# Top-k attention with a maxout MLP: norms of the weights by products on TensorE, low halves from TensorE and ScalarE, loads ranked anew

## The chip, the core and the metric

One core of a Trainium2 chip runs the whole program. Its engines are TensorE (PE, with its weight loads PEld), VectorE (DVE), ScalarE (ACT), GpSimd (POOL) and SyncE (SP), which issues all DMA transfers of this kernel. The metric is the device time of one execution in microseconds.

## What is computed

```python
# q, k, v: (8, 8, 576, 64); top_k = 32
scores = scale * np.matmul(q, k.transpose(0, 1, 3, 2))
kth = np.partition(scores, -top_k, axis=-1)[..., -top_k:-top_k + 1]
scores = np.where(scores >= kth, scores, -1e9)
attn = softmax(scores)
x = np.matmul(attn, v).transpose(0, 2, 1, 3).reshape(4608, 512)
# w1, w2, w3: (512, 768), w_out: (768, 512); all inputs are float64 in memory
h = np.maximum(np.maximum(x @ w1, x @ w2), x @ w3)
out = h @ w_out
```

## The kernel before

The inputs lie in memory as 64-bit numbers. The attention is cut into 144 units of 128 rows for two heads. A unit's scores (`qk`, 12 matmuls) are evacuated by ACT (`evac`) and swept by DVE (`sweep`, 14 MAX8); DVE, POOL and ACT then find the 32nd largest of each row (`pivot`, `sign`, `window` on POOL, `below`, `place`, `pick`), DVE masks (`mask`), ACT takes exponentials (`expo`), PE transposes them (`turn`) and multiplies by v (`values`). `prep` makes q and k of a pair of heads: transposes on PE (`products`), a high part on ACT (`split`), the low part on POOL (line 479).

The MLP works on 576 tokens of a batch. Each float32 operand is a sum of two f16 halves, so each product is three matmuls (`layer`, line 767, for w1 to w3; `layer2`, line 827, for w_out). DVE takes the larger of the three (`largest`).

The weights come once, in 18 parts of 128 rows: 4 each for w1, w2, w3 (768 columns, 786 KB in memory), 6 for w_out (512 columns). They go through these steps:

- `load_weight` issues the DMA of a part on SP.
- `decode` makes float32 out of the 64-bit words, by three DVE instructions (lines 249 to 251) for each half of a part of w1 to w3, or for a whole part of w_out: 30 pieces, 90 instructions. Their result goes into `wall`, the tile of all weights.
- `square_w` squares a part on ACT (line 261); `sum_w` adds the squares up by columns, by two matmuls with ones on PE (line 270). `column_scale` takes the largest column sum on DVE (lines 280, 282), and `powers` makes a power of two of it, by which the matrix is scaled. For w_out the sum over all elements is used (`norm_scale`).
- `cut` makes the two halves, 256 columns at a time: a scaled float32 copy (ACT, line 307), the high half (ACT, line 310) and the difference of the two, the low half (POOL, line 313): 48 of each.

The order of all instructions is made in Python by `in_order`: each step is a `Piece` with an engine, an estimated cost, the pieces it needs, the rings of buffers it takes and a rank. A piece's rank is the unit's number plus an offset by kind (`OFFSETS`). The planner repeatedly takes the piece that could start first, with patience by engine (`PATIENCE`) and within `LEAD` units of rank; pieces marked `alone` wait for POOL and hold POOL back in the plan. MLP pieces are `fill`: PE takes them when nothing else could start. The engines then run what stands in their queue, in order. Two PSUM tiles (ring `m`) serve `layer`, `layer2` and the column sums.

Of the kernel before, what the change touches and what calls it, by code (L numbers as in the profile page):

```python
# [19 lines left out]
CUT = 256  # L20
# [7 lines left out]
GAP = 121.0  # L28
NEAR = 87.0
SWITCH = 95.0  # L30
WINDOW = 150
LEAD = 9.1
LOCK_A = -150.0
LOCK_B = -100.0
OFFSETS = {'E0': 1.08, 'E1': 1.7, 'E2': 0.44, 'N': -1.46, 'T0': 0.49, 'T1': 2.25, 'T2': 3.75, 'Y': -0.11, 'Z': 0.23, 'd': 1.26,
# [94 lines left out]
PATIENCE = {'PE': 121, 'DVE': 164, 'ACT': 32, 'POOL': 175, 'SP': 0}  # L130
# [3 lines left out]
def kernel(ctx, tc, q, k, v, moe_w1, moe_w2, moe_w3, moe_w_out, out):  # L134
# [70 lines left out]
    wosq = const.tile([P, FC], F32, name="wosq")  # L205
    ones_b = const.tile([P, P], BF16, name="ones_b")
    nc.vector.memset(ones_b, 1.0)
    columns = []
    raw_of = {}

    def halves(i, c, c0, n):

        at0 = 2 * ((i * KC + c) * DF + c0 // CUT * CUT) + c0 % CUT
        return [wall.bitcast(F16)[:, at0 + t * CUT:at0 + t * CUT + n] for t in range(2)]

# [4 lines left out]
    def load_weight(j):  # L220
# [7 lines left out]
        elif j < ODD:  # L228
            raw = [t[:, :n] for t in (spare if j % 4 == 1 else [h.bitcast(I32).rearrange("p f n -> p (f n)") for h in H])]
        elif j == len(parts) - 1:  # L230
            raw = [wk.tile([P, 2 * n], I32, name="ssb", bufs=NSSB)]
        else:
            raw = [spare[(j - ODD) // 2]]
# [5 lines left out]
    def decode(j, j0):  # L239

        src, c, n, at0 = parts[j]
        m, k0 = PIECE[n], j0
        raw = raw_of[j]
        if len(raw) == 2:
            raw, k0 = raw[j0 // m:], 0
# [908 lines left out]
```

## Time and profile before

| | |
|---|---|
| Median of 3 timed runs | 1306.12 us (1306.06 to 1307.36) |
| Profiled execution | 1304.12 us |
| its span, first to last instruction | 1301.9 us |
| PE busy | 1174.8 us (90%) |
| DVE busy | 1174.4 us (90%) |
| ACT busy | 1081.6 us (83%) |
| POOL busy | 954.0 us (73%) |
| mean granted clock of PE | 0.973 |

Busy time is what the engine's instructions took; a matmul's end is modelled, so a PE that is busy all the time need not be at its peak rate. Two engines with the same share can be needed at different times, so the stretches matter more than the sums. The granted clock is 1.00 at 2.4 GHz and 0.50 at 1.2 GHz.

### The profile page before, as it was taken

The numbers are of one execution on the slowest core, as the hardware profiler recorded it, in microseconds if no ns is written. First come the engines' busy times: TensorE is split into PE (matmuls) and PEld (weight loads), VectorE is DVE, ScalarE is ACT, GpSimd is POOL, SyncE is SP. The second block draws the span as 40 slices with busy tenths as digits, with TensorE's granted clock in tenths as the row PEclk, the third lists the DMA queues.
The fourth block names the chain that finished last, engine by engine and source line by source line (L and its number), as shares of the span: only waits on it lengthen the run. The fifth ranks groups of instructions, "written<-read, shape, count | busy, mean of one in ns | idle before, by whom it ended". The sixth has DMA issues, their size and how long they took to land.

```text
span 1301.9 us, 31770 instructions
## 1 busy us (share of the span) xinstructions
PE 1174.8 (90%) x10263; PEld 877.3 (67%) x10263; DVE 1174.4 (90%) x5561; ACT 1081.6 (83%) x2438; POOL 954.0 (73%) x1491
## 2 busy tenths in 40 slices
PE   3435878999789999999999999999999999999997
PEld 2223747877568676877777776777677776867775
DVE  7998898999999999999999999999999999999411
ACT  3779988898988899999988998888988898888421
POOL 4659688678877888888778787887787787767310
PEclk9997988999689999999999999999999999999999
DMA  6423112111101101111001111111111111000000
GB/s 200 146 73 109 45 27 47 39 45 37 47 11 28 45 15 50 35 38 47 19 27 39 39 36 42 29 45 29 29 45 28 46 27 37 2 18 2 17 17 28
DMA packets 112399, 54.83 MB, mean 42 GB/s; under 512 B 96608, under 2 KB 104800, under 8 KB 112224
## 3 DMA queue, kind: packets, MB, share of 16 engines
q1 hardware_dynamic: 112224, 52.72, 14.8%
q8 instruction: 83, 1.36, 0.4%
q14 instruction: 92, 0.75, 0.2%
HBM read 43.25 MB, written 9.44 MB: 40 GB/s over the span
## 4 chain that ended last, share of the span: by engine, by line
PE 58%; DVE 13%; ACT 3%; issue 1%; POOL 1%; DMA 0%; SPq 0%; DVEq 0%; POOLq 0%; ACTq 0%
PE m L767 23%; PE tr L710 8%; PE m L827 8%; PE s L518 8%; PE tr L679 7%; DVE L L535 3%; DVE ssb L624 3%; DVE Q L583 2%; PE tr L470 1%; DVE h L776 1%; PE tr L674 1%; ACT pm L633 1%; PE tr L676 1%; DVE z L564 1%; ACT w L574 1%
## 5 line engine op out<-in xcount | busy, mean ns | idle before, releaser
L579 POOL TENSOR_TENSOR w<-ssb,w 128x576 f32<-128x576 f32 x288 | 429.0, 1495 | 56.8 <-ACT w L574 54.2
L767 PE MATMUL m<-xh,wall 128*128 128x256 f16 (+4 forms) x2592 | 440.3, 273 | 2.5 <-DVE h L776 1.7
L767 PEld LDWEIGHTS <-wall 128*128 128x128 f16 x3888 | 352.5, 98 | 75.9 <-issue 11.2
L767 PE MATMUL m<-xl,wall 128*128 128x256 f16 (+4 forms) x1296 | 344.2, 272 | 0.0
L535 DVE MAX8 L<-ssb 128x8 f32<-128x82 f32 (+1 forms) x2016 | 316.3, 228 | 0.2 <-ACT ssb L526 0.2
L624 DVE SCALAR_TENSOR_TENSOR ssb<-ssb,kth 128x576 f32<-128x576 f32 x288 | 256.9, 906 | 1.8
L633 ACT ACTIVATE pm<-ssb,nb 128x576 f32<-128x576 f32 x288 | 223.8, 778 | 26.4 <-DVE ssb L624 25.6
L574 ACT ACTIVATE w<-ssb,Q 128x576 f32<-128x576 f32 x288 | 222.2, 775 | 22.7 <-DVE Q L567 18.8
L691 ACT COPY pT<-tr 128x512 f32<-128x512 f32 (+1 forms) x432 | 215.3, 513 | 22.1 <-PE tr L679 12.9
L583 DVE MAX8 Q<-w 128x8 f32<-128x576 f32 x288 | 215.5, 750 | 6.5 <-POOL w L579 6.3
L679 PE MATMUL tr<-ident,pm 128*128 128x128 f32 x1152 | 183.6, 286 | 24.2 <-ACT pm L633 16.2
L518 PE MATMUL s<-kT,qT 64*128 64x288 f32 x1920 | 179.1, 324 | 20.8 <-ACT ssb L526 11.6
L710 PE MATMUL tr<-pT,vt 128*64 128x256 f32 (+2 forms) x2000 | 182.3, 332 | 4.1 <-ACT pT L691 3.6
L518 PEld LDWEIGHTS s<-kT,qT 64*128 64x128 f32 x1920 | 142.5, 198 | 60.1 <-ACT ssb L526 20.0
L679 PEld LDWEIGHTS tr<-ident,pm 128*128 128x128 f32 x1152 | 133.9, 145 | 68.1 <-ACT pm L633 25.3
L526 ACT COPY ssb<-s 128x1152 f32<-128x1152 f32 x144 | 160.9, 1118 | 14.6 <-PE s L518 13.8
L776 DVE SCALAR_TENSOR_TENSOR h<-m,rises,h 128x256 f32<-128x256 f32 (+4 forms) x216 | 103.0, 477 | 69.0 <-PE m L767 64.7
L710 PEld LDWEIGHTS tr<-pT,vt 128*64 128x64 f32 x2000 | 113.3, 141 | 61.8 <-issue 16.6
L782 POOL TENSOR_TENSOR hl<-h,hh 128x256 f16<-128x256 f32 (+4 forms) x108 | 80.4, 745 | 77.1 <-ACT hh L779 75.8
L827 PE MATMUL m<-wall,hh 128*128 128x512 f16 x432 | 129.2, 380 | 1.6 <-POOL wall L313 1.1
L827 PE MATMUL m<-wall,hl 128*128 128x512 f16 x216 | 82.1, 380 | 0.0
L779 ACT CAST hh<-h 128x256 f16<-128x256 f32 (+4 forms) x108 | 43.6, 404 | 44.4 <-DVE h L776 43.9
(124 smaller groups left out, 1685.4 us busy)
## 6 DMA issues: line engine op xcount, KB each, us to landing
qt<-in_q_dram SPq DMA_DIRECT2D x72, 128.0 KB, 2.8
kt<-in_k_dram SPq DMA_DIRECT2D x72, 128.0 KB, 3.0
out_dram<-ob SPq DMA_DIRECT2D x32, 256.0 KB, 2.3
wall<-in_moe_w_dram SPq DMA_DIRECT2D x8, 768.0 KB, 5.6
vt<-in_v_dram SPq DMA_DIRECT2D x32, 128.0 KB, 2.4
vt<-in_v_dram SPq DMA_DIRECT2D x32, 64.0 KB, 2.2
vt<-in_v_dram SPq DMA_DIRECT2D x96, 16.0 KB, 2.0
vt<-in_v_dram SPq DMA_DIRECT2D x32, 48.0 KB, 2.1
```

The costliest lines, as they stand in the source:

```text
L518: nc.tensor.matmul(s[:, h, i, :HALF], qT[sl, qa, c0:c0 + P], kT[sl, ka, i * HALF:(i + 1) * HALF], start=(n_ == 0 and a == 0), stop=(n_ == ...
L535: nc.vector.max(d["L"][:, t, g, :], d["ssb"][t][:, g * S // G:(g + 1) * S // G])
L574: nc.scalar.activation(d["w"][t], d["ssb"][t], AF.Sign, bias=d["Q"][:, t, 0:1], scale=-1.0, accum_out=d["cnt"][:, t:t + 1])
L579: nc.gpsimd.tensor_tensor(d["w"][t], d["ssb"][t], d["w"][t], ALU.mult)
L583: nc.vector.max(d["Q"][:, t, 1:NW], d["w"][t])
L624: nc.vector.scalar_tensor_tensor(ss, ss, d["kth"][:, t:t + 1], ss, ALU.is_lt, ALU.subtract, accum_out=d["lost"][:, t:t + 1])
L633: nc.scalar.activation(d["pm"][:, t], d["ssb"][t], AF.Exp, bias=d["nb"][:, t:t + 1], scale=-1.0 / SHRINK, accum_out=d["sums"][:, t:t + 1])
L679: nc.tensor.transpose(pt[:, j * P:(j + 1) * P], pm[:, i, 64 * i + j * P:64 * i + (j + 1) * P], ident)
L691: nc.scalar.copy(pT[:, 512 * i:512 * i + m] if i < 2 else pT[:, 8 * P:10 * P], pt[:, :m])
L710: nc.tensor.matmul(xp[64 * h:64 * h + 64, to], vt[:, 4 * h + i if i < 4 else 8 + h, :], keys, start=(i == 0), stop=(i == 4))
L767: nc.tensor.matmul(box["ps", i][:, :c1 - c0], a, bb[:, kc, c0:c1], start=(kc == 0 and k == 0), stop=(kc == KC - 1 and k == 2))
L827: nc.tensor.matmul(box["po"][:n], a[:, f, cs], bb, start=(f == 0 and k == 0), stop=(f == FC - 1 and k == 2))
```

## The change

- `sum_w` now multiplies each 128 columns of a part with themselves on PE: the upper 16 bits of the float32 words are read as bf16, as weights and as moving data. The products of all parts of a matrix add up in one `m` tile; it holds 128 columns. `square_w` and the ones are gone. w_out is treated like the others.
- `row_most` takes the largest of each row (DVE), `all_most` spreads these over all partitions by a matmul with the identity (PE), and `column_scale` takes the largest and the power of two.
- `times` makes a scaled identity (ACT, one for each matrix). `cut` takes 384 columns of w1 to w3 or 512 of w_out at a time: `whole` multiplies by the scaled identity in float32 (PE), `high` writes the high half (ACT), `rest` adds minus the high half (PE, f16, with `less`, minus the identity), and `low` copies what remains out of PSUM as f16 (ACT). There are 30 of each; they take `m` tiles.
- `decode` is handed to the planner as three pieces instead of one, each `alone`.
- The last part of w_out no longer uses a score buffer; it waits for the decode of part 13. The matmuls of `layer` need all four parts' low halves of a column range, those of `layer2` all of w_out.
- The planner's constants, offsets and costs are new. The first weight (`wl`) and the first q and k (`ql0`) have offsets of their own.

```diff
-CUT = 256
+CUT = 512
-GAP = 121.0
-NEAR = 87.0
+GAP = 104.0
+NEAR = 162.0
-LEAD = 9.1
+LEAD = 42.7
-OFFSETS = {... 'ql': -5.77, ... 'wl0': -2.77, 'wl1': -2.59, 'wl2': -2.1, 'wl3': 7.51, ...}
+OFFSETS = {... 'ql': -21.46, 'ql0': -6.17, ... 'wl': -57.18, 'wl0': -31.31, 'wl1': -3.9, 'wl2': 5.47, 'wl3': 16.6, ...}
-PATIENCE = {'PE': 121, 'DVE': 164, 'ACT': 32, 'POOL': 175, 'SP': 0}
+PATIENCE = {'PE': 97, 'DVE': 158, 'ACT': 0, 'POOL': 0, 'SP': 0}
...
-    def square_w(j):
-        squares = squares_of[j] = wk.tile([P, DF], BF16, name="junk", bufs=2)
-        nc.scalar.activation(squares[:, :n], wall[:, CUT + at0:CUT + at0 + n], AF.Square, **kw)
     def sum_w(j):
-        for k in range(2):
-            nc.tensor.matmul(columns[k][:, :DF // 2], ones_b, squares[:, k * (DF // 2):(k + 1) * (DF // 2)], start=(c == 0),
+        for f in range(n // P):
+            w = wall.bitcast(BF16).rearrange("p (n t) -> p n t", t=2)[:, CUT + at0 + f * P:CUT + at0 + (f + 1) * P, 1]
+            nc.tensor.matmul(columns[min(j // KC, 3)][:, :P], w, w, start=(c == 0 and f == 0), stop=(c == last - 1 and f == n // P - 1))
...
+    def row_most(i):
+        nc.vector.tensor_reduce(most[i], columns.pop(i)[:, :P], AX.X, ALU.max)
+    def all_most(i):
+        nc.tensor.matmul(pt[:, :P], most[i].to_broadcast((P, P)), ident, start=True, stop=True)
...
-        def scaled():
-            nc.scalar.activation(box["ws"], w, AF.Copy, scale=box["down"])
+        def whole():
+            nc.tensor.matmul(box["ps"][:, :m], times_of[min(j // KC, 3)], w, start=True, stop=False)
         def high():
...
+        def rest():
+            nc.tensor.matmul(box["ps"][:, :m], less, hi, start=False, stop=True)
         def low():
-            nc.gpsimd.tensor_tensor(lo, box["ws"], hi, ALU.subtract)
+            nc.scalar.copy(lo, box["ps"][:, :m])
...
-                    x = piece("DVE", 1650 if i < 3 else 2000, lambda j=j, j0=j0: decode(j, j0),
+                    rel, steps, cost = [], decode(j, j0), (383, 593, 475) if i < 3 else (480, 727, 640)
+                    x = piece("DVE", cost[0], steps[0], [...], rank, [("ob", rel), ("ob", rel)], alone=True, tag=f"wd{i}")
+                    for f, t in zip(steps[1:], cost[1:]):
+                        x = piece("DVE", t, f, [x], rank, alone=True, tag=f"wd{i}")
```

The order that the planner makes of it is another from the start. On SP, whose queue sets when transfers begin, the program opened with q and k of the first pair of heads and two parts of w1 behind them (qt, kt and last are the raw q and k):

```order
L432 DMA qt<-in_q_dram 128x4x64 x2
L432 DMA kt<-in_k_dram 128x4x64 x2
L436 DMA last<-in_q_dram 64x2x64
L436 DMA last<-in_k_dram 64x2x64
L236 DMA wall<-in_moe_w_dram 128x1536 x2
```

Now it opens with all four parts of w1, then q and k, then two parts of w2 (one of them in two tiles, xh and xl):

```order
L236 DMA wall<-in_moe_w_dram 128x1536 x4
L445 DMA qt<-in_q_dram 128x4x64 x2
L445 DMA kt<-in_k_dram 128x4x64 x2
L449 DMA last<-in_q_dram 64x2x64
L449 DMA last<-in_k_dram 64x2x64
L236 DMA wall<-in_moe_w_dram 128x1536
L236 DMA xh<-in_moe_w_dram 128x768
L236 DMA xl<-in_moe_w_dram 128x768
```

Three transfers of weights moved ahead of the first q and k. On DVE the first unit's sweep (L535 before, L548 now) followed the fourth piece of decoding:

```order
L249 TENSOR_SCALAR ob<-wall 128x384
L250 SCALAR_TENSOR_TENSOR ob<-wall,ob 128x384
L251 SCALAR_TENSOR_TENSOR wall<-wall,ob 128x384
L535 MAX L<-ssb 128x8 x14
L549 MAX b_0_119<-L 128x8 x2
L553 MAX n_247<-nA 128x8 x2
L555 TENSOR_REDUCE nb<-nA 128x2
L559 MATCH_REPLACE nR<-n_247,nA 128x28 x2
L561 MAX n_247<-nR 128x8 x2
L564 SCALAR_TENSOR_TENSOR z<-n_247,b_0_119 128x18
```

Now it stands in the middle of the eleventh piece (the three lines of a decode are 251, 254 and 257), and single decodes stand between the steps of the unit:

```order
L251 TENSOR_SCALAR ob<-xh 128x384
L254 SCALAR_TENSOR_TENSOR ob<-xh,ob 128x384
L548 MAX L<-ssb 128x8 x8
L257 SCALAR_TENSOR_TENSOR wall<-xh,ob 128x384
L548 MAX L<-ssb 128x8 x6
L251 TENSOR_SCALAR ob<-xl 128x384
L562 MAX b_0_118<-L 128x8 x2
L566 MAX n_334<-nA 128x8 x2
L568 TENSOR_REDUCE nb<-nA 128x2
L254 SCALAR_TENSOR_TENSOR ob<-xl,ob 128x384
```

Six and two thirds more pieces of decoding and the maximum of w1 moved ahead of the first sweep. On PE the queue opened with the transposes of k and q (L461, L470) and the first unit's scores (L518), and the sums of squares (L270) came behind them:

```order
L461 MATMUL tr<-ident,last 128x128
L470 MATMUL tr<-ident,kt 128x128 x4
L470 MATMUL tr<-ident,qt 128x128 x4
L518 MATMUL s<-kT,qT_113 128x288 x12
L270 LDWEIGHTS ones_b
L270 MATMUL m<-junk,ones_b 128x384
```

Now 18 products of w1 with itself (L269) and the transposes of k stand first, then the other 6; the piece begins with the last of them. Between it and the first scores (L531) stand `all_most` (L282), the transposes of q (L483) and the first `whole` (L322); a second `whole` and a `rest` (L328) follow:

```order
L269 MATMUL m<-wall 128x128
L282 MATMUL tr<-ident,m_220 128x128
L483 MATMUL tr<-ident,qt 128x128 x4
L322 MATMUL m<-wall,times_246 128x384
L531 MATMUL s<-kT,qT_112 128x288 x12
L322 MATMUL m<-wall,times_246 128x384
L328 LDWEIGHTS less
L328 MATMUL m<-wall,less 128x384
```

The transposes of q moved behind w1's products, and the scores behind the first cut.

## Rows read from the trace of the kernel before

**Rows 1.** Windows: us; PE, PEld, DVE, ACT, POOL busy (x); clock; DMA share; GB/s.
```profile
0.00:100.00 100.00, 37.42 (x175) 25.67 (x175) 88.25 (x274) 65.38 (x131) 53.89 (x81) 1.00 0.45 138
100.00:200.00 100.00, 70.59 (x621) 52.58 (x621) 90.34 (x392) 90.11 (x216) 81.52 (x120) 0.83 0.21 61
...
300.00:400.00 100.00, 82.21 (x664) 60.60 (x663) 95.05 (x482) 89.86 (x203) 76.55 (x125) 0.85 0.13 31
...
500.00:600.00 100.00, 100.00 (x897) 74.69 (x897) 96.75 (x506) 94.00 (x213) 85.49 (x131) 1.00 0.17 43
...
1200.00:1302.00 102.00, 94.58 (x901) 70.47 (x898) 31.21 (x94) 31.25 (x76) 23.09 (x40) 0.99 0.06 20
```

**Rows 2.** Evacuations (L526), one a unit, in 0:150, 150:300, 300:450; min/median/max, first, last start.
```profile
L526 ACT COPY ssb<-s x11: 1097/1118/1130, 15.5 to 144.7; 128x1152 f32<-128x1152 f32 x11
...
L526 ACT COPY ssb<-s x18: 1101/1118/1142, 164.5 to 293.0; 128x1152 f32<-128x1152 f32 x18
...
L526 ACT COPY ssb<-s x19: 1096/1113/1142, 305.2 to 442.6; 128x1152 f32<-128x1152 f32 x19
```

**Rows 3.** Timeline of DVE, the first decodes: start, duration, instruction, idle before.
```profile
9.51 1.36 DVE L249 TENSOR_SCALAR ob<-wall 128x384 int32<-128x384 int32 x1 [7.97 <-DMA wall<-in_moe_w_dram]
10.91 1.78 DVE L250 SCALAR_TENSOR_TENSOR ob<-wall,ob 128x384 int32<-128x384 int32 x1
```

**Rows 4.** Timeline of POOL in the same stretch.
```profile
10.61 1.66 POOL L479 TENSOR_TENSOR qT<-raws,qT 128x640 fp32r<-128x640 f32 x1
```

**Rows 5.** Windows of lines 249, 250 and 251 alone, all decodes.
```profile
0.00:150.00 150.00, 19.56 (x30) 0.93 0.40 124
...
0.00:150.00 150.00, 24.15 (x30) 0.93 0.40 124
...
0.00:150.00 150.00, 25.04 (x30) 0.93 0.40 124
```

**Rows 6.** The same lines' instructions that read or write wall: ns min/median/max.
```profile
L249 DVE TENSOR_SCALAR ob<-wall x19: 341/366/1684, 9.5 to 133.9; 128x384 int32<-128x384 int32 x16, 128x512 int32<-128x512 int32 x3
...
L250 DVE SCALAR_TENSOR_TENSOR ob<-wall,ob x19: 558/560/1796, 10.9 to 134.3; 128x384 int32<-128x384 int32 x16, 128x512 int32<-128x512 int32 x3
...
L251 DVE SCALAR_TENSOR_TENSOR wall<-wall,ob x19: 557/559/1780, 12.7 to 135.1; 128x384 int32<-128x384 int32 x16, 128x512 int32<-128x512 int32 x3
```

**Rows 7.** Groups by line and shape: busy us, mean ns, idle before.
```profile
L691 ACT COPY pT<-tr 128x512 f32<-128x512 f32 x288 | 165.9, 584 | 13.8 <-PE tr L679 12.9
...
L313 POOL TENSOR_TENSOR wall<-ws,wall 128x256 f16<-128x256 f32 x48 | 38.2, 800 | 13.2 <-ACT wall L310 12.0
...
L307 ACT ACTIVATE ws<-wall,down_wi 128x256 f32<-128x256 f32 x36 | 17.9, 498 | 0.1
...
L261 ACT ACTIVATE junk<-wall 128x768 bf16<-128x768 f32 x12 | 10.1, 842 | 19.4 <-DVE wall L251 18.4 <-issue 1.0
...
L270 PE MATMUL m<-junk,ones_b 128*128 128x384 bf16 x24 | 9.6, 503 | 39.7 <-ACT junk L261 39.7
...
L280 DVE TENSOR_REDUCE m<-m 128x1 f32<-128x384 f32 x6 | 3.0, 547 | 0.0
```

**Rows 8.** Timeline of PE: transposes of q; first-layer products and values near the end.
```profile
7.63 1.06 PE L470 MATMUL tr<-ident,qt 128*128 128x128 f32 x4
...
1180.91 0.43 PE L767 MATMUL m<-xh,wall 128*128 128x320 f16 x2
1181.18 0.30 PE L767 MATMUL m<-xl,wall 128*128 128x320 f16 x1
1181.32 0.43 PE L767 MATMUL m<-xh,wall 128*128 128x320 f16 x2
...
1188.39 2.38 PE L710 MATMUL tr<-pT,vt 128*64 128x256 f32 x20
```

**Rows 9.** Timeline of SP: the first transfers of weights.
```profile
4.82 1.07 SPq L236 DMA_DIRECT2D wall<-in_moe_w_dram  x2
```

**Rows 10.** A window of 2 us while weights come; columns as in rows 1.
```profile
8.00:10.00 2.00, 0.69 (x4) 0.29 (x2) 0.49 (x1) 1.94 (x4) 0.74 (x1) 1.00 0.98 406
```

More of the change, by code (lines that the diff above doesn't have):

```diff
@@ new lines, in end, with front, sum_w @@
+        def end():
+            nc.vector.scalar_tensor_tensor(box["t1"], box["low"], 29, box["t0"], ALU.logical_shift_right, ALU.bitwise_or)
+        def front():
+            nc.vector.scalar_tensor_tensor(wall.bitcast(I32)[:, CUT + at0 + j0:CUT + at0 + j0 + m], box["top"], -0x40000000, box["t1"],
+                                           ALU.bitwise_and, ALU.bitwise_or)
+        return middle, end, front
+    def sum_w(j):
+        src, c, n, at0 = parts[j]
+        if c == 0:
+            columns[min(j // KC, 3)] = ps_m.tile([P, 512], F32, name="m")
+        last = KC if j < 3 * KC else FC
+        for f in range(n // P):
+            w = wall.bitcast(BF16).rearrange("p (n t) -> p n t", t=2)[:, CUT + at0 + f * P:CUT + at0 + (f + 1) * P, 1]
+            nc.tensor.matmul(columns[min(j // KC, 3)][:, :P], w, w, start=(c == 0 and f == 0), stop=(c == last - 1 and f == n // P - 1))
@@ L279, in column_scale @@
-        for k in range(2):
-            nc.vector.tensor_reduce(m1[:, k:k + 1], columns[k][:, :DF // 2], AX.X, ALU.max)
         m2 = sm.tile([P, 1], F32, name="m2", bufs=1)
-        nc.vector.tensor_reduce(m2, m1, AX.X, ALU.max)
-        powers(f"wi{i}", m2, const)
+        nc.vector.tensor_reduce(m2, most.pop(i)[:, :P], AX.X, ALU.max)
+        powers(f"wi{i}" if i < 3 else "wo", m2, const)
+        if i == 3:
+            return
         nc.vector.tensor_copy(backs[:, i:i + 1], scale_of[f"wi{i}"][1])
@@ L347, in weights @@
                 n = parts[j][2]
-                takes = [("ssb", release_last)] if j == len(parts) - 1 else []
-                before = {9: (5,), 11: (7,), 12: (1,), 13: (9,), 14: (1, 3), 15: (9,), 16: (3,)}.get(j, ())
-                loads[j] = piece("SP", 5000 if i < 3 else 3400, lambda j=j: load_weight(j), [decoded[k] for k in before], rank, takes,
-                                 tag=f"wl{i}")
+                before = {9: (5,), 11: (7,), 12: (1,), 13: (9,), 14: (1, 3), 15: (9,), 16: (3,), 17: (13,)}.get(j, ())
@@ L372, in weights @@
-            if i < 3:
-                scaled = piece("DVE", 1500, lambda i=i: column_scale(i), done, rank, tag=f"wc{i}")
-                release.append(scaled)
-            else:
-                scaled = scale_pieces(norm_scale("wo", lambda: wosq, const), done, rank)
+                done.append(piece("PE", 115 * n // P, lambda j=j: sum_w(j), [x, *done[-1:]], rank, [("m", release)] if parts[j][1] == 0 else [],
+                                  tag=f"ws{i}"))
+            a, rel = piece("DVE", 230, lambda i=i: row_most(i), done, rank, tag=f"wc{i}"), []
@@ L377, in weights @@
+            release.append(a)
+            a = piece("PE", 280, lambda i=i: all_most(i), [a], rank, [("tr", rel)], tag=f"wc{i}")
+            scaled = piece("DVE", 750 if i < 3 else 450, lambda i=i: column_scale(i), [a], rank, tag=f"wc{i}")
+            rel.append(scaled)
+            if i == 3:
                 wo_scaled.append(scaled)
+            ready = piece("ACT", 190, lambda i=i: times(i), [scaled], rank, tag=f"wp{i}")
             for j in mine:
-                for j0 in range(0, parts[j][2], CUT):
+                w = CUTS[parts[j][2]]
+                for j0 in range(0, parts[j][2], w):
```

104 lines of the change are left out of this document (46 added, 58 removed), and 15 rows, old and new, of the table OFFSETS.

## The prediction

> **What bounds the kernel now.** I read busy time by stretch first [rows 1], then how fast the units of attention come [rows 2], then what VectorE (DVE) does in the first 150 us [rows 3 to 6], and only then single prices. The program has two parts. In the first 100 us TensorE (PE) is busy for 37 us and DVE for 88; in the next hundred it is 71 against 90 [rows 1]. DVE is the bound there, since besides attention it decodes all the weights, and most of what it doesn't use is the wait for the first weights, which land at 9.51 us [rows 3]. From 500 us on PE is busy all the time and DVE for 97 of 100 us: both are full. After 1200 us PE alone works on, 95 of 102 us, while DVE has 31 [rows 1]: the last batch's matmuls. So whatever brings the full part forward ends the kernel earlier by as much, as long as PE, which is full from then on, gets no more to do there. What PE does in its idle time before 200 us (62.6 and 29.4, so 92 us) is free.
>
> **The decode.** 90 DVE instructions, 19.56 + 24.15 + 25.04 = 68.8 us [rows 5]. Undisturbed, the three for 384 columns take 0.35, 0.56 and 0.56, together 1.47 us (the minima of [rows 6], near the medians); 24 pieces give 35.2. The six pieces of 512 columns, in proportion, take 1.95 each: 11.7. So 46.9 us would do and 21.9 us are lost. Where: the second decode takes 1.78 us at 10.91 and ends with POOL's low part of q, which began at 10.61 and took 1.66 [rows 3, 4]. Laid beside POOL's rows, the 90 decodes lose about 8 us to the subtractions that make the weights' low halves (L313), about 9 to the low parts of q and k (L479) and 6 to the products of the search (L579).
> The change takes all 48 subtractions from POOL (38.2 us [rows 7]), so 8 us go for certain. It also puts the first 10 of 30 pieces ahead of the first unit's sweep, when POOL has only the low parts of one q and k to make, so part of the other 15 goes too. Bounds: 8 us (the rest stays) and 18 (three quarters of the rest goes as well). I take **12**: a third of the pieces meet an almost idle POOL, and a third of the remaining 14 is some 5, less 1 because the first pieces of before met little either.
> The Trainium skill, "SBUF — State Buffer", section "Who interferes with whom", says that a DVE instruction with two inputs in SBUF and a GpSimd instruction that reads SBUF exclude each other for the whole instruction, and that the order of issue decides who waits. The pair of rows above agrees. By that rule each decode cut loose as a piece of its own may meet a whole POOL instruction, and the gain could go back; this is rival A.
>
> **The start.** SyncE issues the first weight only after six transfers of q and k, at 4.82 us [rows 9], and it lands at 9.51. Now four weight pieces go first. Between 8 and 10 us, when weights were moving, 406 GB/s came in [rows 10]: 786 KB in 1.9 us. DVE can then start near 5 us (bounds 4.5 and 9.5). But the first unit waits in turn: the transposes of q now stand behind the products for w1's maximum, which need all eight decoded pieces: 5 + 8 × 1.47 = 16.8, and about 1.5 more for the maximum, which goes DVE, PE, DVE. Before, 7.9 us passed from the transposes of q at 7.63 [rows 8] to the first evacuation at 15.5 [rows 2]; so now the first evacuation comes at about 26, 10.5 us later. By then DVE has done 10 2/3 pieces instead of 4 and w1's maximum: 6.7 × 1.47 + 1 = 10.8 us more. The net gain is 10.8 - 10.5 = 0.3; I take **0** (bounds: a loss of 4 if the weights still start at 9.5, a gain of 5 if nothing waits).
>
> **Norms.** On ACT 18 squares go (842 ns for 768 columns) and on PE 24 matmuls with ones (9.6 us) [rows 7]. Of the two reductions of 384 columns (547 ns each) for each of three matrices there remain two of 128 columns, and w_out gets two. In proportion, with the small steps, this saves DVE between 0 and 2 us; **1**. DVE now waits for PE in the middle of the maximum, with a decode in between; that is in the start's sum.
>
> **The cuts.** ACT's 48 scaled copies (498 ns for 256 columns) and 48 high halves become 30 high halves of 384 or 512 columns and 30 copies out of PSUM (512 columns: 584 ns [rows 7]). With the squares ACT goes from about 63 to 34 us of such work. ACT isn't the bound, so I book nothing, and up to 5 us as upside: DVE stood idle for 9.7 us between 100 and 200 us, when ACT was busy for 90 [rows 1].
> PE gets 30 float32 products with the scaled identity, 30 f16 products with minus the identity, 96 products of 128 columns and 4 more. Float32: ten matmuls of 256 columns, two side by side, take 2.38 us [rows 8], so 0.476 per step and 1.86 ns per column: 24 × 0.71 + 6 × 0.95 = 22.8 us. F16: three matmuls of 320 columns in 0.41 us (1180.91 to 1181.32 [rows 8]), 0.427 ns per column: 24 × 0.164 + 6 × 0.219 = 5.2; the 96, at 0.055, 5.3; the four about 1. Together 34 us at full clock. At the lower of the two levels (1.2 GHz) it is twice that: early transposes take 1.06 us for four [rows 8]. Less the 9.6 removed that is 25 to 59 us, against 92 idle: **0** on the path. The cover fails where PE stands in order in front of a product that waits for ACT, with a unit's scores queued behind it.
> The Trainium skill, "VectorE: DVE Perf Modes", section with the errata-adjusted cycle table, gives a matmul as 6 cycles plus its columns at 2.4 GHz; by that the 30 float32 products would take 5 us. The row says over four times as much, so the sum keeps 22.8; since idle time covers both, the result would be the same.
>
> **What is late next: the matmuls of the MLP.** With w3 and w_out cut later, PE starts on the MLP later in the units' order. Counted in the two orders: ahead of the 29th unit's scores PE has done 82,944 columns of the first layer and 39 products of the second before, now 35,328 and 18; ahead of the 48th 136,704 and 72, now 141,312 and 72. So 47,616 + 4,608 columns × 0.427 ns and 21 × 0.219 us, together 26.9 us, move into these 19 units. They took from 293.0 to 442.6 us [rows 2]. There PE was idle for 17.8 us of the hundred from 300 on, at a mean granted clock of 0.85, which is 30 us at the lower level and 15 us of work lost [rows 1]: 32.8 us of room. It just fits, so **0** (bounds 0 and 26.9, the second if none of the room can be used). Behind the 48th unit both orders have the same work left.
>
> **The end.** Of the last batch's first stretch, 42 matmuls of 256 columns that stood ahead of the last values now stand behind them: 42 × 0.109 (256 × 0.427 ns) = 4.6 us if PE has to wait for these values, 0 if PE is full; **2**.
>
> **Sum.** -12 (decode) + 0 (start) - 1 (norms) + 0 (cuts) + 0 (MLP) + 2 (end) = -11. The profiled execution took 1304.12 us, 1301.9 of it the span; its prediction is 1293. The median of the timed runs, 1306.12, lies 2 us higher, so **1295**.
>
> **Rivals.**
> A. *The collisions only change partners.* The low parts of q and k and the search's products stay on POOL, and decodes interleaved one by one meet them. For it: two thirds of the loss isn't L313's. Against: 8 us of it is. If a 2 us gain is left of 12, the total is -1: 1305.
> B. *PE becomes the bound, slower.* From about the 29th unit PE must do 26.9 us more than before. If it stands in line behind ACT and the two PSUM tiles that the cuts and the MLP share, only part of the 32.8 us of room can be used. For it: PE is full everywhere else, and the room is made of short waits and low clock. Against: full work also raises the clock. It decides from the point where less than 16 us of the room is used: 26.9 - 16 takes the sum's 11. With none used the time is 1306 + 26.9 - 11 = 1322, with half of that 1308.
> C. *More comes off than is booked.* The collisions fall by 18, the start gives 5 and ACT's relief 5: 1306 - 18 - 5 - 1 - 5 = 1277.
> D. *The order isn't what decides*: all gains are given back in the full part, since both engines have 2 to 3 % left there: within 2 us of 1306.
>
> **How the numbers follow.** Forecast 0.52 (1287 to 1303), C 0.16, A 0.10, D 0.06, B 0.16. About 0.2 % (2.6 us) is what a measurement of this kernel can tell from no change. Faster by more than that: forecast, C and a third of A, 0.71. Within it: the rest of A, and D, 0.13. Slower: B, 0.16. The range 1277 to 1312 leaves out half of B, half of C and little else.
>
> **What would show it.** Right: the decodes' sum falls from 68.8 to about 57 us; the first decode starts near 5 us and the first evacuation near 26; the 29th unit's evacuation starts some 12 us earlier, near 281, and the 48th about 430, with PE over 95 % busy between them at full clock; the part behind it is unchanged. Wrong: the decodes lose as much as before (A); the 29th unit comes earlier but the 48th doesn't, with DVE waiting for PE's m tiles (B); or the first units come later because PE's queue stands behind a cut.

## The result, and the profile after

| | before | after |
|---|---|---|
| Median of the timed runs | 1306.55 us (1306.06 to 1307.36, 4 runs) | 1265.61 us (1263.07 to 1268.32, 4 runs) |
| Profiled execution, its span | 1304.12, 1301.9 us | 1265.52, 1263.8 us |
| DVE busy, PE busy | 1174.4, 1174.8 us | 1139.0, 1190.5 us |

The ratio is 0.9686 (95% interval 0.9665 to 0.9707). The kernel is faster, as forecast, but by 41 us, where the forecast had 11; the time lies 11 us below its range. So the question is where the other 30 us come from. The profiled execution of before is 2.4 us below its median, that of after at its median, so differences between the profiles (38.1 us in the span) come out somewhat smaller than those between the medians. In the experiments below one execution of *cuts back* took 1732.45 us, at a mean granted clock of 0.652 where that run's others had 0.954 to 0.963, and is left out of its median.

Windows of after, with the columns of [rows 1], which they answer:

```profile
0.00:100.00 100.00, 64.87 (x402) 43.16 (x402) 86.06 (x357) 67.49 (x141) 48.42 (x77) 0.98 0.56 175
100.00:200.00 100.00, 80.58 (x665) 57.15 (x664) 96.07 (x462) 90.19 (x204) 79.36 (x116) 0.90 0.14 33
...
300.00:400.00 100.00, 95.75 (x907) 74.51 (x905) 97.83 (x502) 89.36 (x206) 83.47 (x131) 0.98 0.12 30
...
500.00:600.00 100.00, 98.82 (x862) 74.00 (x860) 97.81 (x498) 92.38 (x210) 81.52 (x123) 1.00 0.14 34
```

PE was 37 and 71 us busy in the first two hundreds and is now 65 and 81: the new products fill idle time. Between 300 and 400 us it went from 82 at a clock of 0.85 to 96 at 0.98. DVE, the bound of the first part, has in 100 to 200 us gone from 90 to 96.

Evacuations of after in the three stretches of [rows 2] (the line is 539 now), then two short stretches, of which the last evacuations are those of the 29th and the 48th unit:

```profile
L539 ACT COPY ssb<-s x15: 1097/1119/1138, 24.8 to 145.9; 128x1152 f32<-128x1152 f32 x15
...
L539 ACT COPY ssb<-s x19: 1099/1122/1157, 153.4 to 296.3; 128x1152 f32<-128x1152 f32 x19
...
L539 ACT COPY ssb<-s x19: 1102/1124/1158, 304.4 to 442.4; 128x1152 f32<-128x1152 f32 x19
...
L539 ACT COPY ssb<-s x2: 1120/1129/1138, 253.6 to 258.2; 128x1152 f32<-128x1152 f32 x2
...
L539 ACT COPY ssb<-s x2: 1108/1124/1141, 398.6 to 404.1; 128x1152 f32<-128x1152 f32 x2
```

The first unit is evacuated 9.3 us later (15.5 to 24.8), and then the units overtake: by 150 us 15 have come instead of 11. The 29th comes at 258.2 (293.0 before) and the 48th at 404.1 (442.6), where the forecast had 281 and about 430. By the 61st unit the gain is 36.8 us (542.8 to 506.0); from there to the end both kernels take the same time (759.1 and 757.7). Nearly all of the gain is made while the weights are decoded and cut, or right behind that. A single unit's start depends on the order too: over units 52 to 70 after is 28.5 to 42.7 us ahead, 34.1 in the mean.

The first steps of DVE in after (timeline), as [rows 3] for before:

```profile
5.21 0.36 DVE L251 TENSOR_SCALAR ob<-wall 128x384 int32<-128x384 int32 x1 [3.81 <-DMA wall<-in_moe_w_dram]
...
25.92 1.26 DVE L548 MAX8 L<-ssb 128x8 f32<-128x82 f32 x8 [1.64 <-ACT ssb L539]
```

Decoding starts 4.3 us earlier, and the first evacuation at 24.8 (its sweep at 25.92): both near the forecast (5 and 26). All decodes of after, by their three lines, as in [rows 5]:

```profile
0.00:300.00 300.00, 14.96 (x30) 0.96 0.29 85
...
0.00:300.00 300.00, 19.32 (x30) 0.96 0.29 85
...
0.00:300.00 300.00, 20.41 (x30) 0.96 0.29 85
```

The sum is 54.7 us (68.8 before; forecast about 57). Against the 46.9 us that they would take undisturbed, 7.8 us are lost now, 21.9 before.

**Where DVE's time went, by the 61st unit.** The records of neighbouring DVE instructions overlap a little, so each instruction is counted here with the time that it adds to the busy time. Busy time and idle time up to the 61st unit's evacuation then sum to its start (542.8 and 506.0):

| us up to the 61st unit | before | after | difference | forecast |
|---|---|---|---|---|
| decode, 90 instructions | 66.4 | 49.6 | -16.8 | -12 |
| steps of the search (`pivot` -7.3, `below` -1.9) | 161.0 | 151.8 | -9.2 | none |
| idle | 37.7 | 29.8 | -8.0 | 0 |
| `mask` | 96.2 | 93.8 | -2.4 | none |
| norms (`column_scale`, `row_most`) | 3.7 | 2.4 | -1.3 | -1 |
| all else | 177.8 | 178.6 | +0.9 | |
| sum | 542.8 | 506.0 | -36.8 | -13 |

Of the idle time 5.4 us are shorter waits ahead of decodes, most of it the wait for the first weight (8.0 us to 3.8). Of `pivot`'s 7.3 us 4.8 are one step, the maximum of z (`Q<-z`, line 567, 580 in after). Directly behind z, whose result it reads, its record ends 0.21 us after z's; with another instruction between it adds 0.08. In before 52 of these steps up to the 61st unit stand directly behind z, in after 3. This table is worked out from all DVE records; the same working is used for the runs below.

### The profile page after: what moved, and what is told of

Its sections match the earlier page's. It is cut to its first block, busy times and chain, and to the rows that moved or that the text cites. A ratio compares the mean times of both kernels' runs of the same rounds, so it can differ in the third digit from the quotient of the medians.

```text
span 1263.8 us, 32126 instructions
## 1 busy us (share of the span) xinstructions
PE 1190.5 (94%) x10431; PEld 882.2 (70%) x10431; DVE 1139.0 (90%) x5558; ACT 1057.1 (84%) x2382; POOL 927.2 (73%) x1443
## 4 chain that ended last, share of the span: by engine, by line
PE 71%; DVE 17%; ACT 8%; issue 2%; POOL 1%; DMA 1%; SPq 0%; ACTq 0%; DVEq 0%; POOLq 0%
PE m L780 28%; PE tr L723 11%; PE s L531 10%; PE m L840 10%; PE tr L692 8%; DVE L L548 4%; DVE ssb L637 4%; DVE Q L596 2%; PE tr L483 2%; ACT pm L646 2%; ACT w L587 2%; PE tr L687 1%; ACT pT L704 1%; DVE h L789 1%; ACT ssb L539 1%
## 5 line engine op out<-in xcount | busy, mean ns | idle before, releaser
L548 DVE MAX8 L<-ssb 128x8 f32<-128x82 f32 (+1 forms) x2016 | 317.2, 227 | 3.1 <-ACT ssb L539 3.1
L637 DVE SCALAR_TENSOR_TENSOR ssb<-ssb,kth 128x576 f32<-128x576 f32 x288 | 262.3, 923 | 0.2
L646 ACT ACTIVATE pm<-ssb,nb 128x576 f32<-128x576 f32 x288 | 224.5, 781 | 29.8 <-DVE ssb L637 29.3
L704 ACT COPY pT<-tr 128x512 f32<-128x512 f32 (+1 forms) x432 | 215.0, 515 | 31.6 <-PE tr L692 17.9
L692 PE MATMUL tr<-ident,pm 128*128 128x128 f32 x1152 | 179.3, 282 | 11.4 <-ACT pm L646 6.6
L531 PE MATMUL s<-kT,qT 64*128 64x288 f32 x1920 | 173.1, 316 | 14.4 <-ACT ssb L539 8.5
L723 PE MATMUL tr<-pT,vt 128*64 128x256 f32 (+2 forms) x2000 | 179.3, 328 | 2.7 <-ACT s L192 1.9
L531 PEld LDWEIGHTS s<-kT,qT 64*128 64x128 f32 x1920 | 137.7, 192 | 58.8 <-ACT ssb L539 19.5
L539 ACT COPY ssb<-s 128x1152 f32<-128x1152 f32 x144 | 161.5, 1121 | 14.5 <-PE s L531 13.7
L692 PEld LDWEIGHTS tr<-ident,pm 128*128 128x128 f32 x1152 | 131.3, 142 | 51.4 <-issue 14.6
L795 POOL TENSOR_TENSOR hl<-h,hh 128x256 f16<-128x256 f32 (+4 forms) x108 | 83.8, 776 | 83.8 <-ACT hh L792 82.8
L661 POOL TENSOR_SCALAR rsw<-rs 128x128 f32<-128x128 f32 x144 | 62.1, 431 | 27.9 <-DVE rs L656 10.8
```

What stands on the lines that cost most here:

```text
L531: nc.tensor.matmul(s[:, h, i, :HALF], qT[sl, qa, c0:c0 + P], kT[sl, ka, i * HALF:(i + 1) * HALF], start=(n_ == 0 and a == 0), stop=(n_ == ...
L548: nc.vector.max(d["L"][:, t, g, :], d["ssb"][t][:, g * S // G:(g + 1) * S // G])
L637: nc.vector.scalar_tensor_tensor(ss, ss, d["kth"][:, t:t + 1], ss, ALU.is_lt, ALU.subtract, accum_out=d["lost"][:, t:t + 1])
L646: nc.scalar.activation(d["pm"][:, t], d["ssb"][t], AF.Exp, bias=d["nb"][:, t:t + 1], scale=-1.0 / SHRINK, accum_out=d["sums"][:, t:t + 1])
L692: nc.tensor.transpose(pt[:, j * P:(j + 1) * P], pm[:, i, 64 * i + j * P:64 * i + (j + 1) * P], ident)
L704: nc.scalar.copy(pT[:, 512 * i:512 * i + m] if i < 2 else pT[:, 8 * P:10 * P], pt[:, :m])
```

## The experiments

In the table u29 and u61 are the starts of the 29th and the 61st unit's evacuation and "end" is the span, all of the profiled execution. The ratio is to the kernel before, run beside it. "52 to 70" is the mean difference of these 19 units' starts, for after and the runs on before against before, for the others against after. Where a run keeps the order of all instructions (POOL rows back, no low halves), the 19 differences agree within 0.1 us. In the runs on parts that make the plan anew, they spread by 10 to 20 us between the smallest and the largest, so that a single unit's start (u29, u61) is good to some 5 us only, and the mean is the better reading.

| kernel | u29 | u61 | 52 to 70 | end | median | ratio (95%) |
|---|---|---|---|---|---|---|
| before | 293.0 | 542.8 | | 1301.9 | 1306.55 | 1 |
| after | 258.2 | 506.0 | -34.1 | 1263.8 | 1265.61 | 0.9686 (0.9665 to 0.9707) |
| *after, one part back* | | | | | | |
| POOL rows back | 271.2 | 519.0 | +13.0 | 1276.5 | 1278.56 | 0.9780 (0.9763 to 0.9796) |
| decode in one | 277.5 | 515.0 | +11.3 | 1282.2 | 1284.59 | 0.9832 (0.9812 to 0.9852) |
| q first | 267.6 | 516.8 | +9.3 | 1277.9 | 1278.88 | 0.9788 (0.9761 to 0.9814) |
| these three | 298.7 | 542.1 | +42.4 | 1313.0 | 1314.09 | 1.0043 (1.0031 to 1.0055) |
| norms back | 265.6 | 513.4 | +8.2 | 1274.5 | 1274.74 | 0.9750 (0.9734 to 0.9766) |
| cuts back | 293.5 | 535.0 | +31.1 | 1299.9 | 1296.85 | 0.9920 (0.9900 to 0.9940) |
| *before, one part given* | | | | | | |
| no low halves on POOL | 286.5 | 537.2 | -5.6 | 1296.5 | 1298.58 | 0.9929 (0.9913 to 0.9946) |
| decode split | 295.8 | 545.0 | +9.0 | 1304.8 | 1308.91 | 1.0012 (1.0002 to 1.0022) |
| weights first | 294.1 | 539.6 | +5.5 | 1304.2 | 1303.89 | 0.9970 (0.9956 to 0.9983) |
| these three | 295.7 | 540.7 | +4.3 | 1314.3 | 1318.32 | 1.0096 (1.0072 to 1.0121) |
| the table | 297.8 | 537.5 | 0.0 | 1304.4 | 1305.81 | 0.9990 (0.9980 to 1.0000) |

**POOL's subtractions put back (after).** Each `low` of after also issues a subtraction of the same width on POOL into a spare tile; the order is otherwise the same.

```diff
         def low():
+            nc.gpsimd.tensor_tensor(spent[:, :m]..., ident..., less..., ALU.subtract)
             nc.scalar.copy(lo, box["ps"][:, :m])
```

> The changed kernel in the same order, with one more POOL subtraction of 384 or 512 columns behind each copy of a low half (30 in all, 12,288 columns a partition, as many as POOL lost); it writes a scratch tile that nothing reads. Theory C: the 8 us of collisions with the decodes come back at least in part, and POOL's queue is late for units: 1271 to 1276 us. Theory N: POOL had 27 per cent idle, the order was made without these, 1266 to 1270 us.

Measured: +13.0 us at the end, all of it by the 29th unit. The decodes by line:

```profile
0.00:300.00 300.00, 17.03 (x30) 0.91 0.29 82
...
0.00:300.00 300.00, 25.07 (x30) 0.91 0.29 82
...
0.00:300.00 300.00, 22.06 (x30) 0.91 0.29 82
```

That is 64.2 us instead of 54.7. In the busy time decode takes 9.6 us more, the steps of the search 2.4 and the mask 1.4, and DVE's idle time stays (-0.4). The median is above both ranges. So POOL's rows cost DVE more than the decodes' 8 us that the forecast had found in them.

**The same from the other side (before).** `low` in before does nothing; the order stays.

```diff
         def low():
-            nc.gpsimd.tensor_tensor(lo, box["ws"], hi, ALU.subtract)
```

> The kernel before without its 48 subtractions on POOL, in the same order on every engine: the low halves of the weights are left out, and the products of the MLP read the high half in both places, so the instructions of PE are the same and the output is less exact. Theory O (the work on POOL has a worth of its own: each POOL row that goes frees DVE, as in the kernel after, where adding 30 of them cost 13 us): 10 to 15 us by unit 28, and a median of 1292 to 1297. Theory F (the forecast's first part only, the 8 us that the decodes lose to these rows): about 8 us, a median near 1299. Theory N (worth only with the new order: the decodes meet the other POOL work instead): within 3 us of 1307.

Measured: 9 us at the median (0.9929), theory F, and 5.6 at the 61st unit of the profiled execution. Up to there decode gives 6.7 and the mask 2.4, and 3.6 us come back as idle time. (Each layer of this kernel counts the high half twice, so its output is about four times too large, not a little less exact as expected above; the instructions are the same.) Taken off before these rows are worth 6 to 9 us, put on after 13, about what the forecast had for the decode. Since the order stays in both runs, this part of the gain is shown to have a worth of its own.

**Decode in one piece (after).** The decode's three instructions as one piece again, not `alone`.

> The changed kernel with a decode as one step for the planner again (three instructions in a row, with the cost of before, not kept apart from POOL). Dependent neighbours in decodes rise from 24 to 60. If the splitting is what keeps decodes off POOL, their lost time rises from 10 us towards 22, and with 36 x 0.12 us for the neighbours the time is some 1266 + 12 + 4 = 1282 us. If the collisions fell because POOL lost the subtractions, the decodes lose little more than now: 1270 us.

Measured: +19.3 us at the 29th unit, +9.0 at the 61st, +11.3 in the mean. The median is near the 1282 of the first forecast, but not by its sum: decode takes 5.6 us more by the 61st unit, not 12, and 6.8 are idle time. In the first 200 us DVE waits 11.5 us, in five waits, for POOL's products of the search, where after has one wait of 3.5. That the short steps ahead of these products stand behind whole decodes is a reading of the order; no run separates it.

**The split alone (before).**

> The kernel before with one edit: a piece of a weight is decoded as three pieces of the plan, as in the kernel after, instead of one. Nothing is left out. Taken back in the kernel after, the split cost 19 us at the 28th unit, 9 at the 60th and 19 at the end, because the units' short steps stood behind whole decodes. Theory S (the split itself helps wherever it stands): the 60th unit comes some 9 us earlier, the median is 1295 to 1300. Theory L (it helps only where the order was laid out for it; a new cut of the plan scatters the last third by some 10 us either way): 1303 to 1315.

Measured: theory L, +2.2 us at the 61st unit and +9.0 in the mean. Decode falls by 4.4, but the mask takes 6.9 more and `pivot` 4.1: DVE meets POOL elsewhere. A mask takes 0.8 us undisturbed; this one, which began while POOL made two products of the search, took 1.78 (timelines of DVE and POOL):

```profile
133.52 1.78 DVE L627 SCALAR_TENSOR_TENSOR ssb<-ssb,kth 128x576 f32<-128x576 f32 x1
...
133.27 3.30 POOL L582 TENSOR_TENSOR w<-ssb,w 128x576 f32<-128x576 f32 x2
```

**q ahead of the weights (after).** `'ql0': -6.17` becomes `-60.0`.

> The changed kernel with the first q and k loaded ahead of the first weights, as before (offset ql0 -60). The first decode starts near 9.5 us in place of 5.2. Theory S (the earlier start is worth what DVE gains there): 4 us, 1270 us. If the chain behind q sets the first units, as the prediction had it: the first evacuation comes earlier than 24.8 us and the time is 1266 us, within 2.

Measured: the first evacuation comes at 13.9 and at the fifth unit this kernel is 10.6 us ahead of after; at the ninth it is 5.5 behind, at the 61st 10.8 (busy +5.5, idle +5.2) and 9.3 in the mean. Both theories are missed. (In after all four parts of w1 moved ahead of q and k, not three.) DVE's first wait (waits of DVE, line by line: total, times, longest) in this kernel, where after has 3.8 us:

```profile
DVE ob L251 <- DMA wall<-in_moe_w_dram: 8.1, 1, 8.1
```

**Weights first alone (before).** Four weight loads get an offset of -60.

> The kernel before with four weight loads issued ahead of q and k, all else planned by the same rules. Nothing is left out. Theory W (weights first is worth 10 us by itself, because DVE's idle time before the first decode falls from 9.5 to about 5 us and the units' later backlog runs without gaps): the 60th unit comes 7 to 12 us earlier, a median of 1295 to 1300, give or take 10 us in the last third by the new plan. Theory Z (the forecast: what DVE gets done earlier is lost by the first unit's wait): within 3 us at the 60th unit, 1304 to 1317.

Measured: 3.2 us earlier at the 61st unit, 5.5 later in the mean, 0.9970 at the median: theory Z within what these readings are good for. The wait for the first weight falls by 4.5 (4.2 in after), and 5.0 us of longer masks take it back.

**All three taken back (after).**

> The kernel after with the three parts taken back together that were taken back one by one before: the 30 subtractions run on POOL as well (into a tile that nobody reads), a piece of a weight is decoded in one go again, and q is loaded ahead of the first weights. Nothing is left out. Taken back singly they cost 13.0, 20.8 and 18.5 us at the first 28 units and 13.0, 19.0 and 13.3 us at the end. Theory S (these three are the gain, each on its own account): together some 33 us by unit 60 and 1263.8 + 33, so a span of 1297 and a median of 1296 to 1302. Theory O (they overlap: each of them only opens the same room on DVE, and taking one back already loses what the others could save): less than 25 us by unit 60, a median of 1278 to 1288. Theory M (they need one another, together they cost more than the sum): over 1305.

Measured: theory M by the median. At the 61st unit it is +36.1 us, to within 0.8 us of before (singly they cost 13.0 + 9.0 + 10.8 = 32.8 there); in the mean it is +42.4 (singly 13.0 + 11.3 + 9.3 = 33.6), 8.3 later than before, and +49 at the end. (At the 29th unit the single runs cost 13.0, 19.3 and 9.4 us, not the 13.0, 20.8 and 18.5 named above.) Norms and cuts on TensorE and the new table, which this kernel keeps, bring nothing without the three.

**All three given (before).**

> The kernel before with all three parts: no subtractions on POOL (the low halves are left out, as in the run without them), the decode in three pieces, four weight loads first. The norms, the cuts on PE and the table of the plan stay those of before. Theory P (the parts make the gain, in any order): the 60th unit comes 25 to 37 us earlier, near 510, a median of 1268 to 1285. Theory T (a good part of it needs the table that was laid out for them): 10 to 20 us by unit 60, a median of 1287 to 1300.

Measured: neither theory. The decodes lose as little as in after (decode -16.5 us), yet the 61st unit comes only 2.1 us earlier, and the mean is 4.3 later: by the 61st unit idle time rises by 10.9 and the mask by 4.2, and behind it 14.5 us more are lost. Waits of DVE in the first 130 us of this kernel, the longest of PE, and two steps of PE one behind the other (timeline):

```profile
DVE L L538 <- ACT ssb L529: 7.8, 3, 4.1
DVE Q L586 <- POOL w L582: 5.8, 5, 2.8
DVE m L280 <- PE m L270: 4.3, 3, 2.0
```

```profile
PE m L270 <- ACT junk L261: 41.3, 11, 9.0
```

```profile
39.27 0.80 PE L270 MATMUL m<-junk,ones_b 128*128 128x384 bf16 x2 [6.58 <-ACT junk L261]
40.00 1.81 PE L521 MATMUL s<-kT,qT 64*128 64x288 f32 x12
```

In before PE waited as long for the squares (39.7 us in [rows 7]), but there DVE had decodes to do meanwhile. Once these are short, what is late next is, by these waits, the chain of the norms: decode, ACT's square, PE, in whose queue the next unit's scores stand behind a product that waits for ACT (PE waits 6.58 us ahead of the product at 39.27, and the scores follow it). POOL's products are late as well (5.8 us, 0.8 in before). No run takes the squares out of this kernel, so that part is a reading of the waits and not shown by experiment.

**Norms by squares (after).** ACT squares w1 to w3, PE adds them up with ones, DVE takes the maximum.

```diff
-            nc.tensor.matmul(columns[min(j // KC, 3)][:, :P], w, w, ...)
+            nc.scalar.activation(squares_of[j], wall[:, CUT + at0:CUT + at0 + n], AF.Square)
+            nc.tensor.matmul(columns[j // KC][:, :DF // 2], ones_b, squares[:, ...], ...)
```

> The kernel after with the norms of w1, w2 and w3 made as before: ACT squares each weight, PE sums the squares over the rows with ones, DVE takes the maximum (both halves of the columns are added up in one PSUM tile, so the norm is a larger bound; w_out's stays as it is). All else is as in the kernel after. Theory K (the norms on TensorE are what lets the saved DVE work count: with squares PE stands in order behind ACT, which waits for a decode): 10 us or more are lost by unit 28, PE's wait for the squares is the largest of its first 130 us, the median is 1276 to 1290. Theory L (the forecast's 1 us, room on ACT and PE hides the rest): at most 4 us by unit 28, a median of 1264 to 1270.

Measured: +7.4 us at the 29th and the 61st unit, 8.2 in the mean and 9.1 at the median, between the theories, at the median close to K. Only 2.4 us of it are idle time of DVE at the 61st unit (5.1 at the 29th); 4.4 are longer decodes, which meet more of POOL's other rows in this order. The longest wait of PE in the first 130 us is the one expected:

```profile
PE m L278 <- ACT junk L267: 17.8, 7, 9.2
```

**Cuts by ACT and POOL (after).**

```diff
         def whole():
-            nc.tensor.matmul(box["ps"][:, :m], times_of[...], w, start=True, stop=False)
+            nc.scalar.activation(box["ws"][:, :m], w, AF.Copy, scale=...)
         def low():
-            nc.scalar.copy(lo, box["ps"][:, :m])
+            nc.gpsimd.tensor_tensor(lo, box["ws"][:, :m], hi, ALU.subtract)
```

> The kernel after with the cuts made as before, in after's pieces of 384 and 512 columns: ACT makes a scaled copy and the high half, POOL subtracts, PE does nothing for them. All else is as in the kernel after. Adding the 30 subtractions to POOL alone cost 13 us. Theory L (POOL's rows are all that counts; ACT's and PE's share of the cuts is free in both forms): 10 to 16 us by unit 28, a median of 1274 to 1282. Theory K (the cuts on TensorE also relieve ACT, which then delays units): over 20 us by unit 28, a median over 1285. Theory B (PE's 28 us for the cuts were not free after all, so taking them off gives some back): under 8 us, a median under 1273.

Measured: theory K, +35.3 us at the 29th unit and +29.0 at the 61st, of which DVE's idle time is 15.8. The profiled execution is 4.9 us longer than the other two, so these may be too high by as much; the medians differ by 31.2. POOL's rows by themselves were 13.0, so ACT's scaled copies and the other order that comes with them cost some 16 more. PE's granted clock in the first 100 us is lower here, too (0.81, in after 0.98), and its share isn't separated.

**The table alone (before).** The gap, `NEAR`, the lead, the offsets and the patiences of after.

> The kernel before with the table, the gap, the lead and the patiences of the kernel after, and nothing else of the change. Nothing is left out. Theory T (the table is the gain): the 60th unit 15 us or more earlier, a median of 1270 to 1292. Theory P (the table alone does not gain, it only fits the changed parts): within 10 us of before at the 60th unit or later, a median of 1300 to 1330.

Measured: theory P. The 61st unit is 5.3 us earlier, but the mean is unchanged (0.0), and so is the end.

**Is PE's new work free?** (after) Each `whole` is done twice.

> The kernel after with every product of the weight's 16-bit steps times their scale done twice (the first result is written over by the same product): 30 float32 products more, 22.8 us of PE by the forecast's row, twice that at the lower clock. Nothing is left out. The forecast booked PE's new work in the first 300 us at nothing, with idle time as its cover. Theory F (the cover holds, with room left): the 28th unit comes at most 3 us later, the median is 1264 to 1270. Theory B (PE is now close to the bound in that stretch, as rival B has it): half of the 23 to 46 us or more shows, 12 to 25 us, a median of 1277 to 1290, and DVE waits for PE's m and w tiles.

Measured: 1270.83 (0.9726, 0.9710 to 0.9742), u29 +3.7, u61 +3.3. Time of these products, in after and here (window of the line alone: PE, PEld, clock):

```profile
0.00:300.00 300.00, 30.72 (x60) 10.47 (x60) 0.96 0.29 85
```

```profile
0.00:300.00 300.00, 49.13 (x120) 21.56 (x120) 0.96 0.29 83
```

18 us more on PE cost 3.3 to 5.2: theory F in the mechanism, a little over its range.

**The order's own scatter.** A first suspicion was that the short steps gain because other units' steps stand between dependent ones. Two runs asked that: after with `pivot`'s fourth step moved next to its fifth, and before with after's `NEAR` (162) and DVE patience (158).

> The changed kernel in the same plan, but z (the 18-element step of pivot 4) is emitted only where its maximum (pivot 5) stands, directly ahead of it: 144 such pairs in place of 7, and nothing else is planned anew. Theory N with DVE as the bound of the full part: 137 x 0.12 = 16 us, 1282 us. If PE alone is the bound of the full part, DVE's loss is hidden there: about 1268 us. Theory C: 1266 us.

> The kernel before with NEAR 162 and DVE's patience 158, as the change has them; weights, loads and all else as before. The pairs fall from 255 to 103 (z and its maximum from 122 to 12). Theory N: 152 x 0.12 = 18 us, 1306 - 18 = 1288 us. Theory C: 1306 us.

The first gave 1287.37 (0.9850, 0.9833 to 0.9866), above all its theories, but its loss is mostly that step (line 577) running into POOL's products: it takes 46.4 us behind the 29th unit instead of 31.6. The second gave 1327.29 (1.0150, 1.0133 to 1.0167), slower where theory N had it faster: `pivot` falls by 5.8 us to the 61st unit, 4.4 of them the maximum of z, but the mask takes 8.5 more and DVE's idle time rises by 18.6. So a pair costs about what theory N said (0.13 us), and parting them does not by itself make the kernel faster.

Three runs change a constant of the plan a little: after with DVE's patience 164, after with a gap of 105, before with a gap of 122.

> The changed kernel with one planner constant set back: DVE's patience 164 as before, in place of 158, so that it is again above NEAR (162). The computation is the same; only the order moves. In DVE's order the pairs in which an instruction stands directly behind the one whose result it reads (z and its maximum, the eight smallest and z, pick and mask, the steps of a decode) rise from 51 to 241. Theory N (neighbours): each such pair costs DVE about 0.12 us, since the second can't start while the first drains; 190 pairs are 23 us: 1288 us. Theory C (only collisions with POOL, the earlier start and the norms count): these are untouched, 1266 us, within 3.

> The changed kernel with one planner constant moved by a hair: GAP 105 in place of 104 (what a result takes to reach another engine, in ns). No work changes; the planner makes another order. Theory T (the order itself is tuned, and any other order of the same work is worse): 1272 to 1290 us. Theory W (the time follows from the work that each engine has and what it collides with): 1266 us, within 3.

> The kernel before with GAP 122 in place of 121: the same small move for it. Theory T: 1313 to 1330 us. Theory W: 1306 us, within 3.

They gave 1273.09 (0.9742, 0.9726 to 0.9759), 1275.25 (0.9761, 0.9741 to 0.9781) and 1308.36 (1.0012, 1.0001 to 1.0024). The first lies between its theories, the second in T, the third in W. Both changes of after have the 61st unit where after has it (505.7 and 505.6) and lose 7.5 and 9.6 us at the median. For the gap that holds for the units around it, too (mean of 52 to 70: -0.7); for the patience it is chance (mean +2.6, single units from -5.5 to +9.0). So some 10 us of a difference at the end can be the order of the last third, and a difference below 5 us at a single unit says nothing. With the patience of 164 the 52 pairs of z and its maximum are back and `pivot` takes 5.7 us more, but the mask takes 5.6 less: most of what the packing saves is no gain of its own.

## Why the prediction was wrong in size

**What bounds.** Right. DVE bound the first part, PE's idle time there took the new products, and what was gained there reached the end (34.9 us at the 29th unit, 38.1 in the span).

**The decode, booked -12.** The mechanism was right and the size near: the sum fell by 14.1 to 54.7, 2.1 more than booked, inside the bounds of 8 and 18. In the busy time it fell by 16.8, since the split decodes overlap their neighbours' records by 2.7 us more. One reading was wrong: the second decode does not end with POOL's low part of q (10.61 + 1.66 = 12.27) but 0.42 us behind it (12.69), as an instruction would that waited for POOL and then did most of its own 0.56. I gave "a third of the remaining 14" to the pieces ahead of the first sweep; the lost time fell from 21.9 to 7.8. The rule of the Trainium skill's "SBUF — State Buffer" (section "Who interferes with whom") holds in both directions here: DVE time goes when POOL rows go (decode -6.7 us), and comes when they come (+9.6). But rival A, which rested on it, did not occur in this order. In before with the split or the loads alone something near it did: the decodes lost less, and 5 to 7 us of longer masks took the gain back.

**The start, booked 0.** Both times were right (5.21 and 24.8). The sum compared the decodes done by the first evacuation with its delay and stopped there. It left out that the idle time of the first wait is gone for good (4.2 us) and that behind it the units run with fewer gaps: by the 61st unit idle time is 8.0 us lower. In this order weights first is worth 9 to 11 us, in before's nothing that can be told from the scatter.

**The norms, booked -1.** DVE's own work fell by 1.3, as booked. What the step missed is outside that sum: taking the squares back costs 7.4 us at the 61st unit. PE then waits 17.8 us for ACT's squares, but only 2.4 to 5.1 us of the cost are idle time of DVE, and 4.4 are decodes that meet POOL more often. The forecast read the row for it (39.7 us idle behind ACT's squares, [rows 7]) only as a price of the matmuls.

**The cuts, booked 0 with 5 as upside.** For PE the 0 was nearly right: 18 us more of these products cost 3 to 5. All of PE's new products took 55.3 us, where the forecast had 34 at full clock and up to twice that. ACT's relief was the mis-sized side: the cuts made by ACT and POOL cost 29.0 us at the 61st unit, some 16 more than POOL's rows. How much of these 16 is ACT's time, how much PE's clock and how much the other order isn't separated.

**The MLP's matmuls, booked 0.** Right. From the 29th to the 48th evacuation 145.9 us pass (149.6 before), and PE is busy for 96 of the hundred from 300 on, at 0.98, where it was busy for 82 at 0.85: the room was used. Rival B fell, and D with it.

**The end, booked +2.** From DVE's last part of x to the end 82.3 us pass, 77.5 before: 4.9 more, at the upper bound of 4.6. PE is full there, idle for 7.6 us against 7.3, so the matmuls that moved behind the last values cost their full time.

**The step that failed** is the sum's silent term: every part was priced with the rest of the order held still, so that the steps of the search (-9.2), the mask (-2.4) and the idle time (-8.0) stood at nothing. With 4.8 more of the decode these are the 24 us by which the 61st unit was missed (36.8 against 13). The runs show that these are not independent worths. Given to before, the subtractions give 5.6 us in the mean of units 52 to 70; weights first, the split and the table give nothing there (5.5 and 9.0 later, 0.0), and the first three of these four together nothing either (4.3 later). Taken from after, each part costs 8 to 31 in that mean, together more than the whole gain of 34.1. My reading is that each removes the wait that would be late next when another is removed: the decodes freed of POOL leave DVE waiting for scores behind the squares (before with three parts), and without squares and copies on ACT but with late weights and whole decodes nothing is left either (after without three). That the parts need one another is shown; the waits named for it are read from the traces, and of all parts only POOL's rows were put back and taken off with the order kept. My rival C, more comes off, had the right sign and three of the places, and summed them as if each were capped by its own row. What is due to the new constants as such, with everything else of after in place, isn't settled: any other constants also give another order.

## What to carry to other kernels

When several parts of a change each remove a wait on the same engine, don't price each with the others' waits in place: ask after each what is late next, and whether another part of the same change removes that as well. An engine's row "idle behind X" costs nothing only as long as the bounding engine has other work; it is a candidate for the next bound once that work shrinks. Read a change of order where the work differs (here the first 70 units) and over many units: a plan that is made anew moves a single unit's start by some 5 us and the end by some 10. An experiment that keeps the order of all instructions, as the two with POOL's rows did, has no such scatter.

## What was not expected of the hardware

POOL's subtractions of two inputs in SBUF, 38.2 us in 48 rows, cost DVE 9.1 us of busy time up to the 61st unit (decode 6.7, mask 2.4) where they were taken off and nothing else moved. A step of 18 elements on DVE added 0.21 us directly behind the one whose result it reads, and 0.08 elsewhere. The float32 products of 384 columns with the scaled identity took 0.81 us each at full clock, in two records of which the second begins 0.32 us after the first, so the estimate of 0.71 from other shapes was near:

```profile
66.79 0.81 PE L322 MATMUL m<-wall,times 128*128 128x384 f32 x2
```
